# Sums of w1's column blocks made in DRAM by adding transfers, and a reordered opening and last output, in a two-layer attention and squared-ReLU kernel

## The chip, the cores and the metric

The kernel runs on one core of a Trainium2 chip. The metric is the device time of one execution in microseconds. The matrix engine is called PE (its weight loads run on a track of their own, PEld), the vector engine DVE, the scalar engine ACT, GpSimd POOL, and SP is the engine whose queue issues nearly all transfers. The 16 DMA engines serve all queues.

## The reference

One block is applied twice to `x` (2048 tokens, 1024 features): local dilated attention and a squared-ReLU feed-forward, each on a layer-normalised input, with residuals and with the same weights in both layers.

```python
x = x + _A_ref(_layernorm(x), A_wqkv, A_wo)              # 32 heads of 32, window of 8, dilation 2
x = x + _B_ref(_layernorm(x), B_w1, B_b1, B_w2, B_b2)    # h = relu(x@w1+b1)**2 ; h@w2+b2, 3584 wide
# ... and both once more
```

Inside `_A_ref`, each token's query is multiplied with the keys of eight tokens (itself and every second one before it, where there is one), a softmax runs over the eight, and the values are summed with its weights; the result goes through `wo`.

## The kernel before

**Units.** The 2048 tokens are cut into four blocks of 512, and the two layers make eight units, `u` = 0 to 7 (unit 0 is the first block of layer 0). A unit goes through `SA` (layer norm and transposition), `SQ` or `SQ7` (q, k, v), `S2` (products of q and k on DVE, sums over a head on PE, exponentials on ACT, weights times v on DVE), `SW` or `SW7` (output projection, residual, second layer norm), `SF1` (first feed-forward matrix, ReLU, square) and `SF2` (second matrix, residual, output).

**Seven products.** Most matrix products are done in 2 by 2 blocks by Winograd's scheme, with seven block products where the plain form has eight. Three of the seven use blocks of the weight as they are (`RAW`: products 1, 2 and 4), and four use combinations of its blocks (`COMB`: products 5, 7, 6 and 3). The moving side has its combinations too (`rhs_combos`, made on DVE for each unit). `product` (L643 on) issues the eight matmuls of one block product; they have line 659. In it, product 1 goes into PSUM bank X; ACT copies X into Y (`seed_first`, L592), and both banks then take further products.

**Where the weight's combinations come from.** They are made once, when a weight is first used, and stored in DRAM scratch for the later units: `keep_wqkv` (DVE line 527) for q, k, v, `keep_w1` (line 676) for `w1`, `keep_w2` (line 453) for `w2`, `keep_wo` for `wo`. For `w1`, whose 3584 columns are seven column blocks `dp` = 0 to 6 (each holds 256 columns of either half), this happens in unit 0, in `SF1_plain`. There block 0 is multiplied in the plain form (lines 1225 and 1229), and blocks 1 to 6 in the seven-product form. For each block the raw weight (two transfers of 512 KB) is loaded, four DVE instructions make the four combinations `tv` in SBUF, SP stores each of them (256 KB) to the scratch tensor `sw`, and the products of unit 0 take the combinations from SBUF (`X<-T,tv` and `Z<-xnB,tv` in the rows). Units 1 to 7 load a block's four combinations from `sw` in one transfer of 1 MB. The order within a block is set by `AT`: product 1 first, then 5, 2, 6, 3, 7, 4, with the blocks staggered by seven places.

**Softmax of unit 0.** `prod` multiplies q and k for eight chunks of features (line 944, one tile `P` each), adds the tiles in a tree of a given depth (line 952), and PE sums the tree's roots over each head (line 959, 4 matmuls per root). The depth is `DEP0 = (2, 2)` for the two halves of unit 0 and 3 for all later units: depth 2 leaves two roots per half, depth 3 one. ACT takes the exponential into tile `e` (line 970). `av` multiplies the weights with v (line 1023) and adds the eight window positions in three steps (line 1030).

**Opening.** The four tiles of unit 0 are loaded in the order 0, 1, 3, 2, tiles 1 and 2 from ACT's queue (`XACT`) and the others from SP's. Tiles 0 and 1 get their statistics on DVE (`ln_first`, lines 787 and 789) and are normalised there (line 784); tiles 2 and 3 (`LNA`) get theirs on ACT (lines 742 and 746). PE transposes them (line 803), DVE copies the first two out of PSUM in two halves each (line 806), and then the first products for q and k start (line 882).

**Last output.** For the very last output tile (`out_tile` with `end`, line 1450) PE computes the two halves of the last bank one after the other, DVE adds the residual to each half, and SP stores each.

**Order of the work.** Every operation is given to a planner (`Plan`) with an engine, an assumed duration, its dependences and a priority. The planner simulates engines, buffers and DMA with assumed costs and issues everything in the order that comes out. `ORDER` is a list of seeds that shift priorities. On the chip, each engine and each queue then works strictly in that order, and an instruction that waits for a semaphore holds all behind it on its engine. Buffers are slots of fixed classes (`K8`, `K4`, `K2`, `K1`: the numbers of 8, 4, 2 and 1 KB slots).

Of the kernel before, what the change touches and what calls it, by code (L numbers as in the profile page):

```python
# [37 lines left out]
XACT = (1, 2)  # L38
# [10 lines left out]
DEP0 = (2, 2)  # L49
# [4 lines left out]
COMB = (5, 7, 6, 3)  # L54
RT = 4
LNA = (2, 3)
# [3 lines left out]
K8, K4, K2, K1 = 12, 5, 12, 8  # L60
# [65 lines left out]
class Plan:  # L126
# [45 lines left out]
    def schedule(self):  # L172
# [19 lines left out]
        def fits(o):  # L192
            if o.mb and len(landed) >= LANES and landed[-LANES] > t + 1e-9:
                return False
# [27 lines left out]
        landed = []  # L222
# [3 lines left out]
        while left:  # L226
            progress = False
            for e in engs:
# [13 lines left out]
                if o.mb:  # L242
                    dma_free = max(dma_free, end) + o.mb / DMA_MBS
                    end = dma_free
                    landed.append(end + o.lat)
# [84 lines left out]
class _Kernel:  # L330
# [20 lines left out]
    def setup(self):  # L351
# [24 lines left out]
        self.b2b = const.tile([128, D], BF, name="b2b")  # L376
        self.b2d = const.tile([128, BLK], F32, name="b2d")
# [10 lines left out]
        todo = {"k": [("k", 0), ("k", 1)], "qv": [("q", 0), ("q", 1), ("v", 0), ("v", 1)], "w1": list(range(self.NDP))}  # L388
        self.orders = {j: interleave(d) for j, d in todo.items()}
# [963 lines left out]
    def SF2(self, u):  # L1353
# [73 lines left out]
        for q in range(2):  # L1427
            add(X[q], q, 1)
# [168 lines left out]
```

## Time and profile before

| what | value |
|---|---|
| median of three runs | 1133.62 us (1131.38 to 1135.53) |
| the profiled execution: its time, and its span | 1133.11 us, 1131.4 us |
| PE busy | 1119.1 us, 99% |
| DVE busy | 991.6 us, 88% |
| ACT busy | 814.4 us, 72% |
| POOL busy | 1.8 us |
| moved by DMA | 362.35 MB, mean 320 GB/s |
| granted PE clock | 1.00 |

The span is the time from the first to the last instruction or transfer of the profiled execution; its time is 1.7 us longer. "Busy" is the union of an engine's instructions. Matmuls are pipelined, so one row's mean duration (273 ns for 256 columns) is longer than the distance from one to the next (0.87 us for eight of them). The profile is of one execution; the table's median is of three others.

### The profile page before, as it was taken

To read this page: it belongs to the slowest core of one execution; us is meant where nothing else is said; L and a number is where in the kernel's file an instruction comes from. 1 tells how busy PE (TensorE), PEld (TensorE's weight loads), DVE (VectorE), ACT (ScalarE), POOL (GpSimd) and SP (SyncE) were. 2 spreads that over 40 slices of the span, in tenths; PEclk is the share of its full clock that TensorE was granted. 3 is DMA by queue.
4 is the path that set the end of the run, shared out by engine and by line. 5 is a ranking of instruction groups with operands and counts; after the bars stand their busy time and mean duration, and the time that the engine had idled before them with its cause. 6 is when DMAs were issued, how large, how long until landed. Compare 5 with 4: busy or idle time off the path is not lost.

```text
span 1131.4 us, 20642 instructions
## 1 busy us (share of the span) xinstructions
PE 1119.1 (99%) x7856; PEld 770.6 (68%) x7903; DVE 991.6 (88%) x1527; ACT 814.4 (72%) x1631; POOL 1.8 (0%) x8
## 2 busy tenths in 40 slices
PE   9999999999999999999999999999999999999998
PEld 6645764678746887468864788557884678845864
DVE  6999999999996999969999699997999799996341
ACT  7747996568975799556994669937798378933961
POOL 0000000000000000000000000000000000000000
PEclk9999999999999999999999999999999999999999
DMA  9956899999899988999879997899969999589881
GB/s 369 288 190 204 269 326 327 337 356 375 345 362 361 330 358 310 297 392 330 355 288 346 399 365 271 296 381 364 395 212 351 374 363 388 197 297 341 340 302 62
DMA packets 137022, 362.35 MB, mean 320 GB/s; under 512 B 67418, under 2 KB 68570, under 8 KB 116570
## 3 DMA queue, kind: packets, MB, share of 16 engines
q1 hardware_dynamic: 136634, 360.50, 90.9%
q8 instruction: 62, 1.02, 0.4%
q10 hardware_dynamic: 288, 0.52, 0.1%
q14 instruction: 38, 0.31, 0.1%
HBM read 314.84 MB, written 31.46 MB: 306 GB/s over the span
## 4 chain that ended last, share of the span: by engine, by line
PE 92%; ACT 5%; DMA 2%; issue 1%; DVE 0%; ACTq 0%; DVEq 0%; SPq 0%
PE X L659 26%; PE X L1382 15%; PE Z L659 13%; PE Z L1382 7%; PE Y L659 7%; PE pq L882 6%; PE py L481 4%; PE Y L1382 4%; PE py L1078 4%; PE X L1149 3%; PE Z L1149 2%; PE lg L959 1%; DMA w<-in_B_w_dram 1%; PE Y L1149 1%; DMA xt<-xs 1%; ACT r L1317 1%
## 5 line engine op out<-in xcount | busy, mean ns | idle before, releaser
L659 PEld LDWEIGHTS <-w 128*128 128x128 bf16 (+1 forms) x4904 | 479.6, 98 | 71.3 <-DMA w<-sw 1.2
L1382 PEld LDWEIGHTS <-r 128*128 128x128 f16 x1183 | 115.7, 98 | 136.5 <-issue 1.7
L1382 PE MATMUL X<-w,r 128*128 128x512 f16 (+2 forms) x784 | 176.1, 377 | 1.6 <-ACT yxa L1051 1.3
L944 DVE TENSOR_TENSOR P<-q,k 128x2048 f16<-128x2048 f16 x128 | 154.3, 1221 | 2.4 <-ACT q L622 0.9
L659 PE MATMUL X<-T,w 128*128 128x256 f16 x1224 | 154.2, 273 | 0.3 <-ACT u L1286 0.3
L1023 DVE TENSOR_TENSOR pr<-pb,v 128x4096 f16<-128x4096 f16 x64 | 146.2, 2293 | 0.5
L952 DVE TENSOR_TENSOR P<-P,P 128x2048 f16<-128x2048 f16 x110 | 133.3, 1215 | 0.1
L1317 ACT ACTIVATE r<-rr 128x1024 f16<-128x1024 f16 x110 | 124.2, 1147 | 0.2
L1030 DVE TENSOR_TENSOR pr<-pr 128x2048 f16<-128x2048 f16 (+1 forms) x128 | 117.7, 947 | 0.0
L659 PE MATMUL X<-TA,w 128*128 128x256 f16 x864 | 107.2, 273 | 0.1
L882 PE MATMUL pq<-xnA,w 128*128 128x256 f16 (+1 forms) x512 | 86.1, 326 | 0.2 <-ACT k L887 0.2
L592 ACT COPY Y<-X 128x512 f32<-128x512 f32 x115 | 70.3, 611 | 19.8 <-PE X L659 15.3
L1296 ACT CAST y<-Z 128x512 f16<-128x512 f32 x110 | 70.3, 655 | 7.3 <-PE Z L659 7.1
L882 PEld LDWEIGHTS <-w 128*128 128x128 bf16 x512 | 49.9, 98 | 32.6 <-issue 0.7
L1300 DVE TENSOR_TENSOR rr<-u,y 128x512 f16<-128x512 f16 x110 | 45.5, 419 | 25.2 <-ACT y L1296 16.6
L1323 ACT ACTIVATE rr<-Y,b1T 128x256 f16<-128x256 f32 x110 | 54.6, 536 | 4.9 <-PE Y L659 4.3
L659 PE MATMUL X<-xnB,w 128*128 128x256 f16 x440 | 56.1, 273 | 0.1
L659 PE MATMUL Y<-xnB,w 128*128 128x256 f16 x440 | 56.0, 273 | 0.0
L614 ACT CAST yq<-Z 128x512 f16<-128x512 f32 x72 | 41.5, 586 | 19.7 <-PE Z L659 19.7
L1323 ACT ACTIVATE rr<-X,b1T 128x256 f16<-128x256 f32 x110 | 55.6, 570 | 0.0
L1051 ACT CAST yxo<-X 128x512 f16<-128x512 f32 x27 | 15.4, 586 | 55.5 <-PE X L1382 55.5
L610 ACT CAST u<-X 128x512 f16<-128x512 f32 x72 | 41.5, 586 | 18.6 <-PE X L659 18.1
(166 smaller groups left out, 1684.6 us busy)
## 6 DMA issues: line engine op xcount, KB each, us to landing
w<-sw SPq DMA_DIRECT2D x49, 1024.0 KB, 9.1
w<-tw SPq DMA_DIRECT2D x56, 896.0 KB, 6.7
w<-in_B_w_dram SPq DMA_DIRECT2D x42, 896.0 KB, 5.3
w<-in_B_w_dram SPq DMA_DIRECT2D x35, 1024.0 KB, 9.8
w<-in_A_wqkv_dram SPq DMA_DIRECT2D x32, 1024.0 KB, 10.1
w<-sqv SPq DMA_DIRECT2D x24, 1024.0 KB, 10.5
w<-in_B_w_dram SPq DMA_DIRECT2D x28, 512.0 KB, 6.3
w<-sk SPq DMA_DIRECT2D x12, 1024.0 KB, 8.2
```

What stands on the lines that cost most here:

```text
L592: self.p.add("ACT", act(512), lambda: self.nc.scalar.copy(Y[:], X[:]), [(X, 0)], [(Y, 0)], UP, name="u")
L659: nc.tensor.matmul(bank[:, a, :], lw[:, k, a * 128:(a + 1) * 128], rhs(k), start=(start and k == 0 and a == 0), stop=(k == 3), skip_group_ ...
L882: nc.tensor.matmul(pq[:, t0 * HB:t1 * HB], w[:, c0 // 2 % 2, kd // 4, kd % 4, c0 % 2 * 128:c0 % 2 * 128 + 128], xnT[:, 2 * t0:2 * t1, kd, ...
L944: nc.vector.tensor_tensor(cur[:], q[:, c, None, hb * HB:(hb + 1) * HB].to_broadcast([128, W, HB]), _win_ap(k[:, c, :], HALO + hb * HB, HB) ...
L952: nc.vector.tensor_tensor(other[:], other[:], cur[:], ALU.add)
L1023: p.add("DVE", dve(4096), lambda pr=pr, ch=ch: nc.vector.tensor_tensor(pr[:], pb[:].unsqueeze(1).to_broadcast([128, 2, W, HB]), _win_ap2(v ...
L1030: nc.vector.tensor_tensor(dst, pr[:, :, 0:n, :], pr[:, :, n:2 * n, :], ALU.add)
L1149: nc.tensor.matmul(bank[q][:], left(j, q), right(j), start=start and j == 0, stop=j == h - 1, skip_group_check=True)
L1296: p.add("ACT", act(512), lambda: nc.scalar.copy(y[:], bank[:]), [(bank, 0)], [(y, 0)], 1.5, name="y")
L1317: p.add("ACT", 0.955, lambda: nc.scalar.activation(out=r2[:, f:f + 2, :].rearrange("p a t -> p (a t)"), in_=r[:].rearrange("p a m t -> p ( ...
L1323: p.add("ACT", 0.36, lambda a=a: nc.scalar.activation(out=r[:, a, 0, :], in_=bank[:, a, :], func=ACTF.Relu, bias=self.b1T[:, f + a:f + a + ...
L1382: nc.tensor.matmul(banks[q][:, lo:hi], left(jj, q), w[:, j, lo:hi], start=(start and jj == 0), stop=(jj == h - 1), skip_group_check=True)
```

## The change

It has these parts.

1. **Signs.** The seven-product scheme is rewritten so that all combinations of weights are sums. Product 1 goes into bank Y, and ACT writes its negative into X (`seed_minus`); some copies on ACT get a scale of -1, and some additions on DVE become subtractions.
2. **Adding transfers.** The host appends to `w1` (and to `wqkv`) six raw blocks per column block, in the order of `SUM`. For the blocks 3, 4, 5 and 6 of `w1` (`DM`), `make` issues four transfers each from POOL's queue: a copy of four raw blocks (1 MB) into the block's scratch, an adding transfer of two blocks (512 KB) onto the first two, one of 256 KB that adds the second to the third, and one of 256 KB that adds the third to the fourth. Each waits for the one before it. The blocks are staggered: step t - i of block i is issued at place t, and a place's transfers also wait for the first transfer of the block two places earlier. All wait for `go`, a small copy on POOL that reads the exponentials of unit 0's first half.
3. **Unit 0's feed-forward.** For blocks 3 to 6 `keep_w1` makes nothing; the products of unit 0 take the combinations from a 1 MB load of the scratch (`combos`). For blocks 0 to 2, and in `keep_w2`, two of the four sums are made by one DVE instruction into a pair tile, which is stored as one (`w1`) or two transfers (`w2`).
4. **DVE additions in `av`.** Six instructions for a pair of tiles become four over the same elements.
5. **Depth.** `DEP0` becomes (3, 3).
6. **Opening.** All four tiles are loaded from SP's queue; tile 2 gets its statistics and its normalisation on DVE, so only tile 3 stays on ACT; the second halves of the transposed tiles 0 and 1 are copied out of PSUM by ACT; the ordering constraints between the first DVE instructions change.
7. **Last output.** The residual is added by PE (a matmul with the identity); the two last halves are then copied out, one by DVE and stored from SP's queue, the other by ACT and stored from ACT's queue.
8. **Slots and order.** `K4` 5 to 6, `K2` 12 to 11, `K1` 8 to 7, and a new `ORDER`.

The core of the diff:

```diff
-XACT = (1, 2)
+XACT = ()
-DEP0 = (2, 2)
+DEP0 = (3, 3)
-COMB = (5, 7, 6, 3)
+COMB = (7, 5, 6, 3)
+SUM = ((0, 0), (1, 0), (0, 0), (0, 1), (1, 0), (1, 1))
+DM = (('w1', 3), ('w1', 4), ('w1', 5), ('w1', 6))
+AHEAD = 2
+POOL_ISSUE, POOL_LAT, MK_COPY, MK_ADD = 0.8, 3.0, 1.15, 1.9
-LNA = (2, 3)
+LNA = (3,)
+CPA = (1,)
+TAIL = True
-K8, K4, K2, K1 = 12, 5, 12, 8
+K8, K4, K2, K1 = 12, 6, 11, 7
...
+    def make(self, blocks, after=()):
...
+            def fn():
+                self.nc.gpsimd.dma_start(dst(), src(), **({} if op is None else {"accum_op": op, "max_dma_last_dim": 4096}))
+            return lambda after: p.add("POOL", POOL_ISSUE, fn, r, w, self.nxt(), after, mb=mb * (MK_COPY if op is None else MK_ADD), name="mk", lat=POOL_LAT)
...
+            return [step(0, 4, lambda: src[:, 0:4096], ()), step(0, 2, lambda: src[:, 4096:6144], (), ALU.add),
+                    step(2, 3, lambda: self.scr[job][d][:, 1].rearrange("p k n -> p (k n)"), [(key, 1)], ALU.add),
+                    step(3, 4, lambda: self.scr[job][d][:, 2].rearrange("p k n -> p (k n)"), [(key, 2)], ALU.add)]
...
+        chains = [rows(d) if job == "w2" else columns(job, d) for job, d in blocks]
+        heads = [after] * AHEAD
+        for t in range(len(chains) + max(map(len, chains)) - 1):
+            for i in range(len(chains)):
+                if 0 <= t - i < len(chains[i]):
+                    op = chains[i][t - i](heads[-AHEAD])
+                    if t == i:
+                        head = op
+            heads.append([head])
...
     def keep_w1(self, dp, w):
...
+        if ("w1", dp) in DM:
+            return self.combos("w1", dp) if dp >= PLAIN1 else None
...
+    def combos(self, job, d):
+        w = Buf("8K", "w", [128, 4, 4, 256], F16)
+        key = (job,) + (d if isinstance(d, tuple) else (d,))
+        self.dma(lambda: w[:], lambda: self.scr[job][d][:], [(key, i) for i in range(4)], [(w, 0)], 4 * 0.256, name="w")
+        return w
...
+    def seed_minus(self, X, Y):
+        self.p.add("ACT", act(512), lambda: self.nc.scalar.activation(out=X[:], in_=Y[:], func=ACTF.Identity, scale=-1.0), [(Y, 0)], [(X, 0)], UP, name="u")
...
+            if DM and u == 0 and hb == GO and EARLYGO:
+                st["go"] = p.add("POOL", 0.2, lambda: nc.gpsimd.tensor_copy(self.go[:], e[:, W - 1, 0:1]), [(e, W // 2 - 1)], [("go", 0)], 0.0, name="go")
...
-                for n in (4, 2, 1):
-                    for pr, ch in prs:
-                        def half(pr=pr, ch=ch, n=n):
...
+                big = prs[0][0]
+                for i, (pr, ch) in enumerate(prs):
+                    op = p.add("DVE", dve(2048), lambda pr=pr, big=big, i=i: nc.vector.tensor_tensor(
+                        big[:, :, 4 * i:4 * i + 4, :], pr[:, :, 0:4, :], pr[:, :, 4:8, :], ALU.add), [(pr, 0)], [(big, 0)], self.nxt(), name="avt")
...
+                half = lambda big, lo, n: big[:].rearrange("p c (g w) t -> p c g (w t)", g=2)[:, :, :, lo * HB:(lo + n) * HB]
+                p.add("DVE", dve(2048), lambda big=big: nc.vector.tensor_tensor(half(big, 0, 2), half(big, 0, 2), half(big, 2, 2), ALU.add),
+                      [(big, 0)], [(big, 0)], self.nxt(), name="avt")
...
+                    if split and half and q and TAIL:
+                        xr = xm[3]
+                        self.pe(1, lambda: nc.tensor.matmul(banks[1][:], self.ident[:], xr[:, 0:BLK], start=False, stop=False, skip_group_check=True),
+                                [(xr, 0)], [(banks[1], 0)], name="pp")
...
+        if end and TAIL:
+            for i in range(2):
...
+                p.add("ACT" if i else "DVE", act(HB) if i else dve(HB, False), lambda a=a, c=c, i=i: (nc.scalar.copy if i else nc.vector.tensor_copy)(o()[:, c], py[:, a]),
+                      [(py, i)], [(xm, (db, i))], -100.0, name="xo")
+                self.dma(lambda c=c: dst[:, c], lambda c=c: o()[:, c], [(xm, (db, i))], [(cell, (db, i))], 0.07, prio=-10.0, eng="ACT" if i else "SP")
+            return
...
         self.S2(0, DEP0)
+        if DM:
+            self.make(DM, [self.state[0]["go"]])
```

More of the change, by code (lines that the diff above doesn't have):

```diff
@@ L192, in fits @@
         def fits(o):
-            if o.mb and len(landed) >= LANES and landed[-LANES] > t + 1e-9:
+            mine = landed[o.eng == "POOL"]
+            n = 4 if o.eng == "POOL" else LANES
+            if o.mb and len(mine) >= n and mine[-n] > t + 1e-9:
                 return False
@@ L244, in schedule @@
                     end = dma_free
-                    landed.append(end + o.lat)
+                    landed[o.eng == "POOL"].append(end + o.lat)
                 out.append((t, len(out), o))
@@ L505, in w2_rhs @@
             lo, hi = half * h, (half + 1) * h
-            r = [(("tw", i), j0) for j0 in range(0, 2 * h, 2) if j0 < hi and j0 + 2 > lo]
+            r = [(("tw", i), half)] if "w2" in DM else [(("tw", i), j0) for j0 in range(0, 2 * h, 2) if j0 < hi and j0 + 2 > lo]
             self.dma(lambda: b[:, :h, :], lambda: self.tw[i][:, lo:hi, :], r, [(b, 0)], h * 0.13, name="w")
@@ L981, in norm, with go @@
                       ec, ec, self.nxt(), name="mask")
+            def go():
+                if DM and u == 0 and hb == GO and not EARLYGO:
+                    st["go"] = p.add("POOL", 0.2, lambda: nc.gpsimd.tensor_copy(self.go[:], ri[:, 0:1]), [(ri, 0)], [("go", 0)], 0.0, name="go")
             if u in DEN:
```

222 lines of the change are left out of this document (135 added, 87 removed), and 16 rows, old and new, of the table ORDER.

## The prediction

> **What bounds the kernel now.** I read the page's busy shares and its chain first, then PE's waits, then a division of the span at PE's first and last useful matmul (columns: stretch, length, then busy time of PE, PEld, DVE, ACT and POOL, granted clock, DMA share, GB/s).
>
> ```profile
> span 1131.4 us, 20642 instructions
> PE 1119.1 (99%) x7856; PEld 770.6 (68%) x7903; DVE 991.6 (88%) x1527; ACT 814.4 (72%) x1631; POOL 1.8 (0%) x8
> PE 92%; ACT 5%; DMA 2%; issue 1%; DVE 0%; ACTq 0%; DVEq 0%; SPq 0%
> ```
>
> ```profile
> 0.00:10.07 10.07, 7.27 (x36) 3.16 (x37) 5.85 (x19) 4.21 (x9) 1.76 (x8) 1.00 0.83 306
> 10.07:1127.20 1117.13, 1111.85 (x7822) 767.41 (x7867) 984.62 (x1506) 810.20 (x1623) 0.00 (x0) 1.00 0.92 321
> 1127.20:1131.40 4.20, 0.00 (x0) 0.00 (x0) 1.09 (x3) 0.00 (x0) 0.00 (x0) 1.00 0.20 62
> ```
>
> ```profile
> PE X L1382 <- ACT yxa L1051: 1.3, 1, 1.3
> PE Z L659 <- ACT rr L1323: 0.9, 1, 0.9
> PE X L659 <- ACT u L1286: 0.3, 1, 0.3
> PE pq L882 <- ACT k L887: 0.2, 1, 0.2
> ```
>
> The chain is PE. Between 10.07 and 1127.20 PE is idle for 1117.13 - 1111.85 = 5.3 us, of which named waits are 1.3 + 0.9 + 0.3 + 0.2 = 2.7; the rest are gaps too short to be listed. DVE, at 88%, ends almost no wait. So a DVE instruction saved is worth nothing by itself. What can be won is PE work, the 10.07 us before the first product, the 4.20 after the last, and part of the 5.3; what can be lost is PE's supply. The profiled execution took 1133.11 us, 1.7 more than its span; the sum starts from it. The median of the runs shown, 1133.62, is 0.5 longer. About 0.3% (3.4 us: 1130.2 to 1137.0 around the median) is what a measurement of this kernel can tell from no change.
>
> **The change part by part.**
>
> ```profile
> 38.55 0.43 PE lg L959 x2
> 50.66 0.86 PE lg L959 x4
> ```
>
> Depth: unit 0 has two halves with two roots of 4 matmuls each, afterwards one root, so 8 of these matmuls go. By the chain's rows one is 0.86 / 4 = 0.215 us: -1.7. PE is never late for work there, so it comes off the end. The price is one more tree addition per half on DVE. The last output adds one matmul with the identity: +0.2.
>
> ```profile
> 5.94 0.69 DVE L787 BATCH_NORM_STATS2 st<-x 128x6 f32<-128x512 bf16 x1 [0.37 <-DMA x<-in_A_x_dram]
> 8.67 1.49 DVE L806 COPY xnA<-pt 128x512 f16<-128x512 f16 x4
> 10.07 5.40 PE L882 MATMUL pq<-xnA,w 128*128 128x256 f16 x48
> 13.37 0.55 DVE L755 TENSOR_SCALAR xn<-x,sm 128x1024 f16<-128x1024 bf16 x1 [3.21 <-ACT sm L750]
> ```
>
> Opening: tile 1's statistics wait 0.37 us for a load that shares the DMA engines with three others; issued second on one queue it should come before the last two, against one more issue ahead of the weights on SP's queue. Four copies at a pitch of 1.49 / 4 = 0.37 us then stand between the transposes and the first product; two go to ACT, beside DVE's, which takes one pitch or a little less off. Together 0 to -1.0, if ACT were slow +0.3; I take -0.6. Tile 2's statistics and norm (about 2.5 us by rows L787 and L755, with its copy) go to DVE, into its idle 3.21 us before 13.37; without that cover, the first P would start later and DVE's work, not PE's.
>
> ```profile
> 1121.13 6.07 PE X L1382 x35
> 1127.23 0.42 DVE xm L1450
> 1127.65 0.33 DVEq L1592
> 1127.98 0.34 DVE xm L1450
> out_dram<-xm SPq DMA_DIRECT2D x2, 64.0 KB, 1.6
> ```
>
> Last output: two DVE instructions stand one behind the other from 1127.23 to 1128.32. On two engines with two queues the second starts with the first and is stored at once: -0.67 by rows 0.33 and 0.34 if ACT's copy is no longer than DVE's 0.42; bounds 0 and -0.8; I take -0.6. The store's 1.6 us stays.
>
> ```profile
> L676 DVE TENSOR_TENSOR tv<-w x14: 679/688/695, 100.7 to 151.8; 128x1024 f16<-128x1024 bf16 x14
> L1030 DVE TENSOR_TENSOR pr<-pr 128x2048 f16<-128x2048 f16 x64 | 77.1, 1214 | 0.0
> L1030 DVE TENSOR_TENSOR pr<-pr 128x1024 f16<-128x1024 f16 x64 | 42.4, 681 | 0.0
> L1030 DVE TENSOR_TENSOR o<-pr 128x512 f16<-128x512 f16 x64 | 25.3, 417 | 0.3 <-PE Z L659 0.3
> ```
>
> DVE: 16 combinations of 0.688 are no longer made, -11.0 in unit 0. In `av` two instructions of 0.681 become one of 1.214, and two of 0.417 one of 0.681: 0.30 saved for each of 32 groups, -9.6 over the kernel. The pairs and the deeper tree (+2.4) cancel roughly. Some 18 us less in all, where PE waits for nothing: 0 directly. It lets tiles reach ACT and PE earlier, and DVE is the engine that the planner must fit PE's work around. With that and a new order I take 1.0 of the 5.3 us of gaps: bounds -2.7 (all named waits gone) and +3 (twice as many; a new order meets the chip's durations as any other does, the named waits here being what the old order missed).
>
> Signs: scale -1 is in the same ACT instruction, and the moved seed has the same place; at worst an instruction of 0.5 us becomes 0.6. ACT is 72% busy and waits for PE oftener than PE for it: 0. SP no longer issues 16 stores, and issues 4 loads: 0.
>
> **The adding transfers.** POOL issues no transfer before, so their cost is bounded by rows of others (issues with size and time to landing; then PE's demand).
>
> ```profile
> w<-in_A_wqkv_dram SPq DMA_DIRECT2D x32, 1024.0 KB, 10.1
> sw<-tv SPq DMA_DIRECT2D x28, 256.0 KB, 3.9
> 39.56 2.05 ACT L970 ACTIVATE e<-lg 128x512 bf16<-128x512 f32 x4
> 129.56 1.04 PE L659 MATMUL Z<-T,tv 128*128 128x256 f16 x8
> 153.07 1.04 PE L659 MATMUL Z<-T,tv 128*128 128x256 f16 x8
> ```
>
> ```profile
> 43.00:57.00 14.00, 14.00 (x71) 6.63 (x70) 14.00 (x17) 8.24 (x19) 0.00 (x0) 1.00 1.14 307
> 57.00:70.00 13.00, 13.00 (x66) 6.31 (x65) 13.00 (x13) 7.20 (x14) 0.00 (x0) 1.00 0.54 198
> 70.00:85.00 15.00, 15.00 (x71) 6.77 (x70) 15.00 (x17) 5.74 (x11) 0.00 (x0) 1.00 0.49 175
> 85.00:100.00 15.00, 14.89 (x70) 6.82 (x70) 15.00 (x21) 11.33 (x25) 0.00 (x0) 1.00 0.26 79
> 100.00:113.00 13.00, 13.00 (x109) 9.17 (x108) 13.00 (x23) 9.52 (x22) 0.00 (x0) 1.00 1.00 348
> ```
>
> The start is the end of unit 0's first exponentials, 41.6, and one tree addition later with depth 3: about 43. Four blocks staggered by one place need seven places. The deadlines: the two rows of PE are the first product with a combination of block 3 (129.56) and of block 6 (153.07). The load before them lands in some 10 us, so block 3 must be done by 119, four places after 43 (19 us each), and block 6 by 143, seven places (14.3 us each). A place lasts at least what a store of 256 KB takes, 3.9, and, if a 1 MB transfer is always in it, 10.1; an addition that reads its target back could double that to 20. I take 8, nearer to the 1 MB row, because a 1 MB copy is in four of the seven places and the engines are half free: the last sum is there at 43 + 56 = 99. In volume, four blocks are 8.4 MB, or 12.6 with the additions' targets read back; at the 400 GB/s that loads reach, the five stretches leave 1.3 + 2.6 + 3.4 + 4.8 + 0.7 = 12.8 MB. So it fits before 113, hidden under PE's work on unit 1's q and k, without much room if the readback counts in full. Cost 0; ends 0 and +10.
>
> On DMA: Bandwidth & Descriptors, section "Issuing engines are not separate DMA queues", the Trainium skill says that transfers from SP, ACT and GpSimd end up on the same 16 DMA engines and interleave. By that rule, loads under way between 43 and 57, where the share is 1.14, would be slowed by the copies, and those between 57 and 100 hardly; by the rows, the sum stays as it is unless the copies also hold back the block loads of 100 to 113, which is the late chain below.
>
> **Sum:** -1.7 + 0.2 - 0.6 - 0.6 - 1.0 + 0 = -3.7; 1133.1 - 3.7 = 1129.4.
>
> **The rivals.**
>
> *The gaps stay or grow.* The certain part is -1.7 + 0.2 - 0.6 - 0.6 = -2.7, and a new order with gaps as long as before or up to 3 us longer gives 1130.4 to 1133.4: no change that can be told. For it: four waits in the old order came although PE is dense everywhere. Against it: DVE is lighter by 18 us.
>
> *The chain of adding transfers is late (slower).* Place: SP's queue at the first or last of the four combination loads. SP holds behind that load every later load of unit 0's feed-forward and unit 1's x tiles, until POOL's transfer has landed; PE starves once its loaded buffers are used. It decides from 14.3 us a place, and each us above costs up to 7 at block 6: 15.4 us a place bring 1129.4 + 7.7 = 1137.1, the edge of slower; 20 us would bring some 40. For it: the share of 1.14 at the start, 1.00 after 100, and places with up to 2 MB in four transfers at once. Against it: 57 to 100 is half empty, and 8 us is little more than half of 14.3.
>
> *The additions in `av` lose their rate.* The new views have four dimensions and could run at double the time, 2.4 instead of 1.214 for three of a group's four: about +3.4 us in each of 32 groups. In units 0 and 1, where DVE is at 100% (stretches above), 8 groups make +27 against 14 saved, and PE would wait for about 13: 1142. Against it: the innermost runs are 256 to 512 elements, no shorter than in the rows quoted, which are strided in tile and window too.
>
> **How the numbers follow.** The forecast, faster by more than 0.3%: 0.52. Gaps: 0.20, no change. A late chain: 0.20, of which 0.05 stays below 1137. Lost rate: 0.03, slower. Others (ACT's scaled copies late, slots short): 0.05, slower. So faster 0.52, same 0.25, slower 0.23. Low end: all bounds at their best, -1.7 + 0.2 - 1.0 - 0.8 - 2.7 = -6.0, 1127.1. High end: a late chain just past its point of decision, 1138. The forecast's own range is 1127.1 to 1130.2.
>
> **What would show it.** Right: 64 matmuls on line 959 instead of 72; first product before 10.07, near 9.5; the two last copies starting together and the span's tail under 4.20; POOL's last addition landing near 99 and in any case before 119 for block 3 and 143 for block 6; no PE wait on a scratch load between 120 and 160; the merged additions at 1.2 and 0.7 us; PE's idle time between first and last product near 4.3. Wrong: an SP queue that waits tens of us for POOL's transfer, loads of 43 to 57 landing far above 10 us with PE waiting, or new waits for ACT across the later units, where no part of the change but signs, slots and order is at work.

## The result and the profile after

The changed kernel is slower. Its median is 1148.08 us (1142.30 to 1150.19, six executions), the kernel before, measured beside it, took 1134.39 us (six executions). The ratio is 1.0117 with a 95% interval of 1.0102 to 1.0132, so about 13.3 us on 1134. The forecast was 1129.4 us, in a range of 1127.1 to 1138.0. The profiled execution took 1148.25 us.

From the page of the kernel after, its span, the busy shares, the chain that ended last, and the row of POOL's queue `q0` (packets, MB, time as a share of 16 DMA engines' span):

```profile
span 1146.5 us, 20510 instructions
PE 1121.5 (98%) x7850; PEld 770.1 (67%) x7896; DVE 982.8 (86%) x1441; ACT 815.4 (71%) x1626; POOL 14.6 (1%) x25
q0 software_dynamic: 2304, 8.39, 3.2%
PE 78%; DMA 10%; DVE 6%; ACT 3%; issue 1%; SPq 0%; DVEq 0%; ACTq 0%
```

DVE's work fell from 991.6 to 982.8 us, about half of what was forecast, and ACT's stayed. The chain is no longer PE nearly alone: 10% of it is DMA, where it was 2%. The span divided at PE's first and last product (columns as in the prediction):

```profile
0.00:9.51 9.51, 7.17 (x35) 3.08 (x36) 6.44 (x20) 4.80 (x10) 1.76 (x8) 1.00 0.76 261
9.51:1142.84 1133.33, 1114.30 (x7815) 767.00 (x7860) 975.95 (x1421) 810.19 (x1616) 12.88 (x17) 1.00 0.95 325
1142.84:1146.45 3.61, 0.00 (x0) 0.00 (x0) 0.42 (x1) 0.37 (x1) 0.00 (x0) 1.00 0.23 73
```

Both ends got shorter, 9.51 instead of 10.07 and 3.61 instead of 4.20. Between them PE is idle for 1133.33 - 1114.30 = 19.0 us, where it was 5.3. Its waits name most of that; these are the ones used below (in all, times, longest):

```profile
PE pq L965 <- DMA xnA<-xn: 8.0, 1, 8.0
PE Y L740 <- DMA w<-in_B_w_dram: 2.5, 2, 1.9
PE Y L740 <- ACT X L672: 2.1, 2, 1.1
PE pq L965 <- DMA w<-in_A_wqkv_dram: 1.2, 1, 1.2
PE Z L740 <- DMA w<-sw: 0.2, 1, 0.2
```

The last row is the sums that the adding transfers make: PE hardly waits for them. It waits once, for 8.0 us, for a transposing transfer that the prediction didn't speak of: the fourth and last tile of unit 1's normalised tokens (`xnA<-xn`, from SP's queue), and then for the raw blocks of `w1`. Three views around the first of these: stretches of 5 us, two of the kernel before and then three of the kernel after; SP's, POOL's and PE's instructions of the kernel after in order of time; and the time from issue to landing of this transposing transfer, in the kernel before (9.6) and after (18.8).

```profile
45.00:50.00 5.00, 5.00 (x27) 2.39 (x25) 5.00 (x6) 3.85 (x10) 0.00 (x0) 1.00 1.28 140
55.00:60.00 5.00, 5.00 (x24) 2.25 (x23) 5.00 (x5) 3.58 (x7) 0.00 (x0) 1.00 1.08 387
```

```profile
50.00:55.00 5.00, 5.00 (x29) 2.65 (x27) 5.00 (x9) 2.41 (x5) 1.45 (x3) 1.00 1.38 296
55.00:60.00 5.00, 1.01 (x6) 0.29 (x3) 5.00 (x8) 0.62 (x2) 0.00 (x0) 0.91 1.10 35
60.00:65.00 5.00, 0.97 (x3) 0.43 (x4) 5.00 (x4) 0.00 (x0) 0.72 (x2) 0.50 1.08 402
```

```profile
45.14 6.29 SPq L849 DMA_TRANSPOSE xnA<-xn  x1
50.19 1.26 POOL L447 DMA_DIRECT2D sw<-in_B_w_dram  x2
64.03 6.23 PE L965 MATMUL pq<-xnA,w 128*128 128x512 f16 x16 [8.02 <-DMA xnA<-xn]
64.28 1.40 POOL L447 DMA_DIRECT2D sw<-in_B_w_dram  x2 [12.83 <-DMA sw<-in_B_w_dram]
```

```profile
xnA<-xn SPq DMA_TRANSPOSE x1, 9.6
```

```profile
xnA<-xn SPq DMA_TRANSPOSE x1, 18.8
```

SP issues the transposing transfer at 45.14, POOL its first two copies of 1 MB at 50.19. Both are done together at about 64. From 55 to 60 the DMA engines are recorded as busy all the time (1.10) and move 35 GB/s. That isn't a bandwidth that is shared; it is a stretch in which almost nothing moves. A transposing transfer moves little by itself too, but not for as long: in the run without transfers below, the stretch of this transfer is 54 to 56, with 141 and 97 GB/s, and in the kernel before 45 to 50 has 140 GB/s. When PE has waited, its clock is granted at 0.50 (60 to 65), so that the first 16 matmuls take 6.23 us; a run below shows sixteen of them in 3.62.

### The profile page after: what moved, and what is told of

Read it like the earlier page. It is cut to its first block, busy times and chain, and to the rows that moved or that the text cites. A ratio compares the mean times of both kernels' runs of the same rounds, so it can differ in the third digit from the quotient of the medians.

```text
span 1146.5 us, 20510 instructions
## 1 busy us (share of the span) xinstructions
PE 1121.5 (98%) x7850; PEld 770.1 (67%) x7896; DVE 982.8 (86%) x1441; ACT 815.4 (71%) x1626; POOL 14.6 (1%) x25
## 3 DMA queue, kind: packets, MB, share of 16 engines
q0 software_dynamic: 2304, 8.39, 3.2%
## 4 chain that ended last, share of the span: by engine, by line
PE 78%; DMA 10%; DVE 6%; ACT 3%; issue 1%; SPq 0%; DVEq 0%; ACTq 0%
PE X L740 17%; PE X L1481 13%; PE Z L740 12%; PE Y L740 12%; PE Z L1481 6%; PE py L552 4%; DMA w<-in_B_w_dram 4%; PE pq L965 4%; PE Y L1481 3%; PE X L1243 3%; PE py L1172 2%; DMA xnA<-xn 2%; DVE P L1035 1%; PE Z L1243 1%; DVE P L1027 1%
## 5 line engine op out<-in xcount | busy, mean ns | idle before, releaser
L740 PEld LDWEIGHTS <-w 128*128 128x128 f16 (+1 forms) x5032 | 491.8, 98 | 79.0 <-DMA w<-in_B_w_dram 3.7
L740 PE MATMUL X<-T,w 128*128 128x256 f16 x1288 | 162.5, 273 | 0.1
L740 PE MATMUL Y<-xnB,w 128*128 128x256 f16 x880 | 110.2, 273 | 4.6 <-DMA w<-in_B_w_dram 2.5
L1119 DVE TENSOR_TENSOR pr<-pr 128x2048 f16<-128x2048 f16 x64 | 78.1, 1220 | 0.1
L1395 ACT ACTIVATE y<-Z 128x512 f16<-128x512 f32 x110 | 70.3, 657 | 5.4 <-PE Z L740 5.2
L740 PE MATMUL Y<-xnA,w 128*128 128x256 f16 x576 | 73.8, 273 | 0.0
L672 ACT ACTIVATE X<-Y 128x512 f32<-128x512 f32 x91 | 55.5, 610 | 19.4 <-PE Y L740 19.1
L690 ACT ACTIVATE u<-X 128x512 f16<-128x512 f32 x72 | 42.9, 597 | 19.9 <-PE X L740 18.7
L695 ACT ACTIVATE yq<-Z 128x512 f16<-128x512 f32 x72 | 42.6, 596 | 18.3 <-PE Z L740 18.0
L740 PE MATMUL Z<-T,w 128*128 128x256 f16 x424 | 54.8, 273 | 0.2 <-DMA w<-sw 0.2
## 6 DMA issues: line engine op xcount, KB each, us to landing
w<-sw SPq DMA_DIRECT2D x53, 1024.0 KB, 10.5
w<-in_A_wqkv_dram SPq DMA_DIRECT2D x32, 1024.0 KB, 10.5
```

Of the source, the lines that this page charges most:

```text
L672: self.p.add("ACT", act(512), lambda: self.nc.scalar.activation(out=X[:], in_=Y[:], func=ACTF.Identity, scale=-1.0), [(Y, 0)], [(X, 0)], U ...
L740: nc.tensor.matmul(bank[:, a, :], lw[:, k, a * 128:(a + 1) * 128], rhs(k), start=(start and k == 0 and a == 0), stop=(k == 3), skip_group_ ...
L1119: op = p.add("DVE", dve(2048), lambda pr=pr, big=big, i=i: nc.vector.tensor_tensor(big[:, :, 4 * i:4 * i + 4, :], pr[:, :, 0:4, :], pr[:, ...
L1395: p.add("ACT", act(512), lambda: nc.scalar.activation(out=y[:], in_=bank[:], func=ACTF.Identity, scale=by), [(bank, 0)], [(y, 0)], 1.5, na ...
```

## The experiments

Two theories stood at the start. **A:** the loss is the collision, packets of a second queue between those of a transposing transfer. **B:** the loss is volume: the adding transfers, with their targets read back, take more of the DMA engines than is free before unit 0's feed-forward needs its loads. Others came up on the way: the half clock, and the reordered opening. In all edits but the last two the order of the work, and so the seeds' plan, stays that of the kernel after, apart from the operations that the text says are moved. Differences in us below are ratios against the kernel before, measured beside each run, times 1134.

**No transfers at all.** This kernel leaves out the sums of blocks 3 to 6: unit 0 and all later units load block 0's sums in their place, so sizes and counts stay. The work of every engine but POOL stays as well.

```diff
-                self.nc.gpsimd.dma_start(dst(), src(), **({} if op is None else {"accum_op": op, "max_dma_last_dim": 4096}))
+                pass
...
+        e = 0 if (job, d) in DM else d
```

> The changed kernel in the same order, but POOL issues none of the 16 copies and adding transfers; the loads of the sums of blocks 3 to 6 take block 0's sums instead, which DVE makes in unit 0, so the products of those blocks are with the wrong weights while sizes and counts stay. Theory A (the transfers are the cause): no wait above 1 us near 56, full clock throughout, and the 4.1 us idle at 121 to 136 go too: 1148.2 - 8.0 - 2.8 - 4.1 = 1133. Theory B (the new order is the cause): 1145 or more, with the wait near 56 still there.

Measured: 1134.91 us, ratio 1.0005 (0.9994 to 1.0017), +0.6 us. So the adding transfers cost 13.3 - 0.6 = 12.7 us, which is all of the loss, and the rest of the change gains nothing that can be told. So the forecast of a faster kernel would have failed without the transfers too; that is taken up below with the opening.

**The chain begun behind the transposing transfer.** POOL's small copy `go` reads the last transposed tile of unit 1 instead of the exponentials, and the transfers are issued after it.

```diff
+    held = [o for o in order[:at + 1] if o.name in ("go", "mk")]
+    keep = [o for o in order[:at + 1] if o.name not in ("go", "mk")]
...
+    return keep + held + order[at + 1:]
...
-                st["go"] = p.add("POOL", 0.2, lambda: nc.gpsimd.tensor_copy(self.go[:], e[:, W - 1, 0:1]), [(e, W // 2 - 1)], [("go", 0)], 0.0, name="go")
+                st["go"] = p.add("POOL", 0.2, lambda: nc.gpsimd.tensor_copy(self.go[:], self.state[1]["xnA"][:, 3, 0, 0:1].bitcast(BF)), [(e, W // 2 - 1)], [("go", 0)], 0.0, name="go")
```

> The changed kernel with its planned order kept, except that the small copy on POOL and the adding transfers behind it are issued behind the last transposing transfer of unit 1's input, and the small copy reads that transposed tile, so that the first block copy starts when it has landed. Theory A: the wait of 8.0 us and the half clock after it (2.8 us lost) come from the two block copies meeting that transposition; both vanish, the transposing transfer lands in about 10 us instead of 18.8, and what the adding transfers cost later (4.1 us idle at 121 to 136) stays or grows, since the sums end later: 1137 to 1143. Theory B: the new order itself runs out of work at 56, whatever the copies do: the wait stays within 2 us of 8.0 and the time at 1146 to 1150.

Measured: 1141.37 us, 1.0066 (1.0051 to 1.0081), +7.5 us. Of this kernel, the stretch of the former wait and the one of the block loads, its two largest waits, and the landing of its transposing transfers; then the stretch of the block loads in the run without transfers:

```profile
55.00:60.00 5.00, 5.00 (x29) 2.57 (x28) 4.63 (x8) 1.98 (x4) 1.80 (x3) 1.00 1.22 282
100.00:140.00 40.00, 34.77 (x245) 22.25 (x243) 34.70 (x48) 22.57 (x48) 4.06 (x5) 1.00 0.78 235
PE Y L750 <- DMA w<-in_B_w_dram: 3.8, 4, 1.5
PE Y L750 <- ACT X L682: 2.9, 2, 1.8
xnA<-xn SPq DMA_TRANSPOSE x2, 10.6
```

```profile
100.00:140.00 40.00, 39.88 (x307) 28.49 (x305) 40.00 (x55) 29.12 (x60) 0.00 (x0) 1.00 0.44 144
```

The wait at 56 is gone, with PE busy throughout and the clock at 1.00, and the last two transposing transfers land in 10.2 and 11.1 us (10.6 is their median). What stays is 5.2 us of idle PE between 100 and 140, for raw blocks of `w1` and for ACT's copies behind the products that they delay. The DMA engines are full where the blocks are loaded: their share is 1.04 to 1.07 in each of five stretches from 57 to 125, where it is 0.41 to 0.92 without transfers. Both theories hold a part.

**The same transfers without adding.** As above, but every transfer is a plain copy of the same size, so the kernel leaves out the sums (the scratch holds raw blocks).

```diff
-                self.nc.gpsimd.dma_start(dst(), src(), **({} if op is None else {"accum_op": op, "max_dma_last_dim": 4096}))
+                self.nc.gpsimd.dma_start(dst(), src(), **{})
```

> The run with the late start, with the 12 adding transfers replaced by plain copies of the same size, so blocks 3 to 6 are multiplied with raw column blocks instead of sums. Theory A (an addition costs the DMA engines about twice a copy's time, and this crowds the loads between 80 and 120): the software queue's share falls from 3.2% to about 1.9%, the chain's last landing moves from about 122 to 105, and PE's idle time at 100 to 140 falls from 5.2 us to below 2: 1137. Theory B (the copies alone crowd the loads, or waits in the chain do): at most 1 us less.

Measured: 1134.83 us, 1.0003 (0.9994 to 1.0013). The 7 us are gone with the adding, more than Theory A had forecast (1137). POOL's queue in the late kernel, then in this one, and this one's stretch from 100 to 140:

```profile
q0 software_dynamic: 2304, 8.39, 3.1%
```

```profile
q0 software_dynamic: 1792, 8.39, 2.1%
100.00:140.00 40.00, 39.88 (x305) 28.43 (x303) 40.00 (x55) 29.42 (x62) 1.05 (x2) 1.00 0.58 200
```

The bytes counted are the same. As a recorded time of all 16 engines, the plain copies take 2.1% of 1131.2 us = 23.8 us, 2.8 us per MB. With adding it is 3.1% of 1139.8 = 35.3 us. Half of the bytes (4.19 MB) are copies in both, 11.9 us, so the adding half takes 23.4 us, or 5.6 us per MB: twice a copy. In the section "Rules for kernel authors" of DMA: Bandwidth & Descriptors, the Trainium skill says that an accumulating transfer reads its destination and writes it later; the doubled time agrees with that. So B is shown, with its size: 6.9 us over the kernel without transfers, and the same bytes as copies cost nothing that can be told. One thing is not separated: `max_dma_last_dim` goes with the adding, so this run has fewer packets too (1792 instead of 2304), and how much of the doubled time is the adding and how much the larger number of packets stays open.

**Two plain copies alone**, in the place of the first two transfers and nothing after them, once from POOL's queue and once from ACT's (the four blocks use block 0's sums, as without transfers).

```diff
-                self.nc.gpsimd.dma_start(dst(), src(), **({} if op is None else {"accum_op": op, "max_dma_last_dim": 4096}))
+                if op is None and w[0][0] in (("w1", 3), ("w1", 4)):
+                    self.nc.gpsimd.dma_start(dst(), self.scr["k"]["k", 0][:].rearrange("p i k n -> p (i k n)"))
...
+        e = 0 if (job, d) in DM else d
```

> The run without transfers, plus two plain DRAM to DRAM copies of 1 MB (stored sums of k, no change of type, into scratch that nobody reads) issued by POOL where the changed kernel issues its first two block copies; the products of blocks 3 to 6 take block 0's sums. Theory A (copies from a second queue beside the transposing transfer): the last transposing transfer of unit 1's input lands in 15 us or more, DMA falls to some 40 GB/s for several us while its share stays at 1, and PE waits 5 to 9 us near 56: 1140 to 1147. Theory B (it takes the change of type or the adding transfers behind): landing near 10 us, no wait above 2 us, 1133 to 1136.

> As the run with two plain copies from POOL, but the two copies are issued from ACT's queue at the same place in the order. If any second queue beside the transposing transfer does it: the same slow stretch near 40 GB/s and a PE wait of 5 to 9 us, 1140 to 1147. If it takes POOL's software queue: landing near 10 us and 1133 to 1137.

Measured: POOL's queue 1145.89 us, 1.0096 (1.0066 to 1.0125); ACT's 1145.70, 1.0092 (1.0047 to 1.0137). So 2 MB of copies cost 10 us by themselves, and it isn't POOL's kind of queue that does it. The first ratio rests on two executions only, and the four of the second lie between 1140.8 and 1152.3. First the copies from POOL, PE's wait and a stretch, then those from ACT:

```profile
PE pq L967 <- DMA xnA<-xn: 8.4, 1, 8.4
55.00:60.00 5.00, 1.23 (x7) 0.39 (x4) 5.00 (x9) 0.85 (x2) 0.00 (x0) 0.87 0.03 14
```

```profile
PE pq L967 <- DMA xnA<-xn: 13.5, 1, 13.5
55.00:60.00 5.00, 1.31 (x7) 0.44 (x5) 5.00 (x8) 0.92 (x2) 0.00 (x0) 1.00 0.28 76
50.26 1.20 ACTq L448 DMA_DIRECT2D sw<-sk  x2
```

The signature is that of the kernel after: the same wait, the transposing transfer landing in 18.8 us (POOL) and 23.6 us (ACT) where it takes 10.9 without transfers, and a stretch of 5 us with 14 or 76 GB/s. How busy the engines count in it differs (0.03, 0.28, 1.10), so that column can't tell a stall from work here; the bytes moved can.

**The same two copies from SP's own queue**, behind the transposing transfer. `go` and the copies are moved behind it as in the late chain; against the run from POOL's queue, the copies' line is:

```diff
-                    self.nc.gpsimd.dma_start(dst(), self.scr["k"]["k", 0][:].rearrange("p i k n -> p (i k n)"))
+                    self.nc.sync.dma_start(dst(), self.scr["k"]["k", 0][:].rearrange("p i k n -> p (i k n)"))
```

> The run without transfers, plus the two plain 1 MB DRAM to DRAM copies of the runs two_pool and two_act, issued from SP's queue directly behind unit 1's last transposing transfer (blocks 3 to 6 take block 0's sums). Theory A (the transposing transfer is slowed by packets of another queue, between its own): on one queue the copies follow it, it lands in about 10.6 us and PE does not wait for it: 1134 to 1137. Theory B (two copies of 1 MB at this place cost by their volume): 1140 or more.

Measured: 1135.39 us, 1.0012 (0.9995 to 1.0028). Of this kernel, the transposing transfer, the copies' issue, the stretch behind it, and the median landing of the last two transposing transfers:

```profile
45.81 5.38 SPq L861 DMA_TRANSPOSE xnA<-xn  x1
54.10 1.20 SPq L458 DMA_DIRECT2D sw<-sk  x2
55.00:60.00 5.00, 5.00 (x29) 2.58 (x28) 4.65 (x7) 2.04 (x5) 1.06 (x1) 1.00 0.94 341
xnA<-xn SPq DMA_TRANSPOSE x2, 10.3
```

The copies are issued before the transposing transfer has landed (10.9 us after 45.81, at 56.7), yet they do no harm: same bytes, nearly the same place, another queue, 9 us less. It also excludes that the 2 MB would be too much there. So it is shown that copies on a second queue beside the transposing transfer cause the loss. That their packets go between its packets is the likely way, and no trace shows it. And one reservation stays: these copies come four microseconds later than those of POOL and ACT, behind four other transfers of SP's queue, so the run doesn't separate the queue from the time at which the copies move.

**Ordinary loads on a second queue.** No transfers, and the two loads of `wo` for unit 0, which SP issues between its transposing transfers, go out from ACT's queue.

```diff
+    held = [o for o in order[:at] if getattr(o.fn, "on_act", False)]
...
+    return order[:at] + held + order[at:]
```

> The run without transfers, with the two 1 MB loads of wo for unit 0 (HBM to SBUF) issued from ACT's queue beside unit 1's last transposing transfer, where SP issues them ahead of it in the other runs. If packets of any transfer on a second queue slow the transposition: landing at 14 us or more and a PE wait of 3 us or more, 1138 or more. If it takes copies from DRAM to DRAM: landing near 10 us or earlier, 1133 to 1136.

Measured: median 1143.74 us, 1.0079 (1.0054 to 1.0105), but in two lumps: two of eight executions took 1133.4 and 1135.9, six 1142.6 to 1146.1. The profiled one is the 1133.4, and shows no wait on `xnA`; its loads were issued at 45.08 and landed in 10.4 us. So moving two loads into SBUF to a second queue mostly costs the same 10 us, and sometimes nothing. No slow one was profiled, so that it was the same wait is likely and not shown, and what decides stays open. In the fast one the transposing transfer landed in 11.9 us with the loads beside it: a second queue alone doesn't do the harm each time.

**The half clock.** Forty matmuls on a tile of ones ahead of unit 1's first product keep PE busy over the wait.

```diff
+                    for _ in range(40):
+                        nc.tensor.matmul(pq[:], g, g[:, None, :].to_broadcast([128, 4, 128]), start=True, stop=True)
```

> The changed kernel with 40 matmuls of ones (512 columns, 8.6 us at full clock) ahead of unit 1's first product, in the bank that this product then overwrites. If the half clock of 10.24 us at 59.5 to 69.7 follows PE's idle time: the granted clock stays 1.00 and 16 matmuls of line 965 behind the wait take 3.5 us instead of 6.2: 1148.2 - 2.8 + 0.6 = 1146. If it has another cause (the DMA traffic, say): the clock still falls, 1148 to 1149.

Measured: 1149.91 us, 1.0145 (1.0128 to 1.0162). By the ratios that is 3 us more than the change, with intervals that just overlap, where 2 us less had been expected. The clock did stay at 1.00 there:

```profile
60.00:70.00 10.00, 10.00 (x48) 4.55 (x47) 6.92 (x5) 2.15 (x5) 2.76 (x4) 1.00 1.04 335
56.13 8.81 PE L969 MATMUL pq<-ones 128*128 128x512 f16 x40
64.78 3.62 PE L971 MATMUL pq<-xnA,w 128*128 128x512 f16 x16
100.00:140.00 40.00, 34.93 (x204) 19.39 (x203) 30.83 (x42) 21.12 (x48) 3.25 (x4) 0.91 1.00 288
```

The 16 matmuls take 3.62 us, not 6.23, so the half clock follows from the idle time before it. In "What's actually happening" of TensorE: Matmul & The Clock Gate, the Trainium skill says that an idle window of some 3.4 us halves the clock; the 8.0 us of idle and the 0.50 agree. But PE is idle for 5.1 us between 100 and 140 all the same. The same products begin 1.9 us earlier than in the kernel after at 101, and 2.35 us later at 144: between them PE waits 2.1 us for a normalised tile and 2.3 for raw blocks of `w1`, whose loads are issued 1.2 to 1.3 us later than in the kernel after, and the clock falls to 0.83 between 110 and 130.

**The opening.** Tiles 1 and 2 go back to ACT's queue, ahead of its table load, once in the kernel after and once in the one without transfers.

```diff
+        order.insert([i for i, o in enumerate(order) if o.name == "x"][3] + 1, tab)
...
-            (self.nc.sync if eng == "SP" else self.nc.scalar).dma_start(o if cast is None else o.bitcast(cast), src())
+            (self.nc.sync if eng == "SP" and not on_act else self.nc.scalar).dma_start(o if cast is None else o.bitcast(cast), src())
```

> The changed kernel with input tiles 1 and 2 issued from ACT's queue again, ahead of the table load, all else in the same order. Theory A: the weights leave SP's queue 0.9 us earlier and PE's wait of 1.24 us for them at 12.20 goes, less what tile 1 loses by sharing: 1147.2, with the first product between 9.5 and 10.1. Theory B: the weights' arrival is set by the volume ahead of them, not by the issue: 1148.2.

> The run without transfers (blocks 3 to 6 take block 0's sums), with input tiles 1 and 2 issued from ACT's queue ahead of the table load. In the run without transfers PE idles 2.24 us between 10 and 20, most of it for the weights. Theory A (one queue for all four tiles delays the weights): the idle time between 10 and 20 falls below 0.8, the first product moves from 9.5 to about 10, and the time falls by 1 to 1.5: 1133.6. Theory B (volume): no difference, 1134.9.

Measured: with the transfers 1150.70 us, 1.0144 (1.0120 to 1.0168), above what either theory gave; there the transposing transfer landed in 21.3 us and PE waited 10.9 us for it, so the run says nothing of the opening. Without them 1134.47, 1.0001 (0.9990 to 1.0012), to be set beside the kernel without transfers at 1.0005: the intervals overlap, no gain can be told. The stretch from 10 to 20 in the kernel before, in the one without transfers (with PE's wait), and in that one with ACT's queue:

```profile
10.00:20.00 10.00, 10.00 (x101) 9.00 (x99) 5.58 (x7) 9.84 (x26) 0.00 (x0) 1.00 1.02 399
```

```profile
10.00:20.00 10.00, 7.76 (x79) 6.66 (x77) 6.30 (x9) 5.60 (x16) 0.00 (x0) 1.00 1.03 411
PE pq L966 <- DMA w<-in_A_wqkv_dram: 1.8, 1, 1.8
```

```profile
10.00:20.00 10.00, 9.30 (x91) 8.04 (x90) 8.17 (x13) 7.57 (x20) 0.00 (x0) 1.00 1.03 408
```

By 20 us PE has begun 83 of the products for q, k and v (`pq`, 0.11 us each) before, 64 without transfers, 73 with ACT's queue, and 72 in the kernel after. (PE's busy time of the first 10 us is mostly products on a tile of ones, and says nothing.) The new opening begins sooner and then waits for weights; with the old queues back it waits less and begins later, at 10.76. As two executions with the same opening differ by 8 products (64 and 72), what the queues alone do isn't shown.

**Fewer blocks, and none, planned anew.** To see the parts without the transfers in a kernel that leaves nothing out, and half of the volume, two versions were planned again with the same seeds, both with the old opening: no blocks by adding transfers, and blocks 5 and 6 alone, begun late.

```diff
-XACT = ()
+XACT = (1, 2)
...
-DM = (('w1', 3), ('w1', 4), ('w1', 5), ('w1', 6))
+DM = ()
...
-LNA = (3,)
+LNA = (2, 3)
...
```

> The changed kernel without any adding transfer (DVE makes the sums of all six blocks, as before the change) and with the opening of before (tiles 1 and 2 from ACT's queue, tile 2 normalised on ACT, DVE's copies and constraints as before), planned anew with the same seeds. Theory A (transfers cost 13, the other parts are worth their matmuls and the shorter tail): 8 matmuls less, 1 more and 0.6 off the tail give -2.1 against before, 1131 to 1133, if the new plan's gaps are like before's. Theory B (what the other parts save is lost in gaps of any order not searched for): 1134 to 1138.

> The changed kernel with only blocks 5 and 6 made by adding transfers, begun behind unit 1's last transposing transfer, DVE making the other blocks' sums, with the opening of before, planned anew with the same seeds. Theory A (the late start costs by volume: 36 us of DMA time do not fit, 18 do): no PE wait on raw weights between 100 and 140 above 1 us, and the time within 2 of the run without transfers and the opening of before. Theory B (any adding transfer beside the loads delays them): half of the late run's 6.5 us remain, 1137.

Measured: 1175.42 and 1175.58 us, both 1.0359 (1.0335 to 1.0383). These runs failed as experiments, and they decide between the theories of neither. In the first, PE's largest waits are many short ones behind ACT (7.0 us in 5, 6.3 in 5), and the transposing transfer is issued at 52.97, so that PE waits for that too, with no second queue in play. That seeds found for one set of operations are an arbitrary order for another, and that this costs the 40 us, is the likely reason and not shown; no part of the change can be read from it.

No kernel beat the one before. The best one that still makes the sums in DRAM is the late chain, at 1.0066.

## Why the prediction was wrong

**The step that failed is "Cost 0; ends 0 and +10", the price of the adding transfers.** It took them to be hidden under PE's work. They cost 12.7 us, beyond its own upper end. Two mechanisms make it up, each seen by itself: the collision with the transposing transfer (10.3 us more with POOL's two copies than without), and the adding itself (6.9 us more with the late chain than without). As ratios they add up to 17.2, more than 12.7. The traces, where the order of PE's work is the same, show how the two follow each other. One group of 16 transpositions on PE (`pt`) stands between the first products of the feed-forward. Without transfers, in the late chain and in the kernel after it begins at (first number):

```profile
118.33 1.06 PE L885 MATMUL pt<-ident,xn 128*128 128x128 f16 x16
124.86 1.21 PE L894 MATMUL pt<-ident,xn 128*128 128x128 f16 x16
132.52 1.22 PE L884 MATMUL pt<-ident,xn 128*128 128x128 f16 x16
```

The last group of 8 transpositions before it, ahead of the first product that needs a block of `w1`, begins at 102.26, 103.96 and 111.99. So in the kernel after PE is 9.7 us behind at the group of 8, from the collision, and 14.2 at the group of 16: 4.5 come between, from the volume. In the late chain it is 1.7 and 6.5, and 4.8 come between. The volume thus costs nearly the same with and without the collision, and the 1.7 were lost before: that execution had a granted clock of 0.91 in its first 20 us and had begun 47 of the products `pq` where the one without transfers had 64. These are single executions (the spans differ by 15.1 us, 1146.5 and 1131.4); so the shares are about 10 and about 5 us, and no closer than that.

*The collision.* The prediction asked what the transfers would do to loads and to volume, and never which transfers in flight at 43 to 57 had PE's next products behind them. The trace of before held it: a transposing transfer is issued on SP's queue at 47.84 and lands in 9.6 us, at 57.4, and a group of products on `xnA` begins at 57.63, so there was hardly any slack. The Trainium skill's rule that it cited (DMA: Bandwidth & Descriptors, "Issuing engines are not separate DMA queues") says that the queues interleave on the same engines. It points the right way, and the prediction listed "loads of 43 to 57 landing far above 10 us with PE waiting" as a sign of being wrong; that is what came, on a transfer that was no load. But sharing doesn't give the size. Two copies need 5.9 us of all engines (2.1 MB at 2.8), and beside them the transposing transfer landed 7.9 (POOL) and 12.7 us (ACT) later than without; and from SP's queue the same copies cost nothing that can be told. In the section "Rules for kernel authors" of DMA: Bandwidth & Descriptors, the Trainium skill says that a transpose next to ordinary DMAs needs nothing. The row there is about what has to be serialized, and the runs here show a price in time.

*The volume.* The prediction found 12.6 MB to fit into 12.8 "without much room", and counted that as hidden. The doubt was the right one: the adding half takes twice the time of a copy, and all sixteen transfers together take 36.7 us of all engines in the kernel after (3.2% of 1146.5). In the prediction's own five rows, the share free from 57 to 113 is 13 x 0.46 + 15 x 0.51 + 15 x 0.74 + 0 = 24.7 us. So it overflows by 12 us, and plain copies (23.8) just fit, as the run without adding shows. In the changed order the share free from 57 to 125, by the run without transfers, comes to 26.2 us, and says the same. Free GB/s had counted 1.3 MB in the stretch at 1.14, where no engine was free.

**The late-chain rival** put the loss at the right object and the wrong place: SP held by sums that come late. A place took about 10.5 us, not 8 (seven from 50.19 to the last landing at 123.7, 8.8 us after the issue at 114.91), under the 14.3 from which it would decide. SP's queue waited for none of these transfers between 75 and 165, and PE waited 0.2 us on `w<-sw`. The deadlines held, and what was late was everything else that used the DMA engines. The start, forecast at 43, came at 50: the new order ends unit 0's first exponentials at 49.6, where they ended at 41.6 before, and the prediction took the old order's time for them, with one tree addition more.

**The sum's other terms.** The depth: 64 matmuls on `lg` as said. The rows are of the kernel after: that group, the additions in `av`, the two last copies, and the weights' first loads.

```profile
L1042 PE MATMUL lg<-P,grp 128*128 128x512 f16 x64 | 19.4, 379 | 0.0
L1119 DVE TENSOR_TENSOR pr<-pr 128x2048 f16<-128x2048 f16 x64 | 78.1, 1220 | 0.1
L1124 DVE TENSOR_TENSOR pr<-pr 128x2048 f16<-128x2048 f16 x32 | 39.1, 1222 | 0.2
L1126 DVE TENSOR_TENSOR o<-pr 128x1024 f16<-128x1024 f16 x32 | 22.0, 688 | 0.4 <-PE X L740 0.3
1142.86 0.42 DVE L1553 CAST xm<-X 128x256 bf16<-128x256 f32 x1 [0.70 <-PE X L1481]
1143.32 0.37 ACT L1553 CAST xm<-X 128x256 bf16<-128x256 f32 x1 [1.62 <-DVE xm L1553]
2.67 4.67 SPq L438 DMA_DIRECT2D w<-in_A_wqkv_dram  x8
```

The additions in `av` keep their rate (1.22 and 0.69), so that rival fell. The last output: 3.61 instead of 4.20, the -0.6 taken, but not by the way given, so the size is luck: ACT's copy still follows DVE's (1143.32, released by it) instead of starting beside it. The copies end 0.85 us after the last product where they ended 1.12 after it, and the other 0.3 is behind the copies.

The opening, taken at -0.6, is a term with the wrong sign in these traces. The first product did come 0.56 us sooner. But the prediction counted "one more issue ahead of the weights"; it is two tiles moved to SP's queue, and the weights start at 2.67 where they started at 1.72. PE then waits for them, 1.2 us here and 1.8 in the kernel without transfers, and by 20 us it is 11 and 19 products `pq` behind before, 1.2 and 2.1 us at 0.11 each. With the depth and the identity at -1.5, the tail at -0.6 and the opening at +1.2 to +2.1 the sum is -0.9 to 0.0, and the kernel without transfers measures +0.6 (-0.7 to +1.9). The gaps, taken at -1.0, gave nothing that shows in the time. In the kernel without transfers PE is idle for 4.5 us between its first and last useful product, 2.2 of them from 10 to 20; the 5.3 of before is from records that lack some 47 matmuls (7856 beside 7903 weight loads), so the two can't be set against each other closely. DVE became lighter by 8.8 us (991.6 to 982.8), not by some 18: the additions in `av` save 144.8 - 139.2 = 5.6 us by the groups' busy times, not 9.6, and tile 2's norm, which moved to DVE, had been left out of that sum. Nothing here contradicts that it is worth nothing directly: the kernel without transfers, with DVE as light, gained nothing that can be told.

## What to carry to other kernels

Before a transfer is moved to an idle engine's queue, look for a transposing transfer in flight at that time and for who waits at its end; here two copies behind it in the same queue, and copies begun after it had landed, cost nothing that can be told. Cost a transfer by the time it takes on the DMA engines (an adding one took twice a copy here) against the share that is free in the stretch where it must be done, and a rival found "without much room" isn't worth 0. Parts of a change whose order comes from a search can only be told apart with that order kept.

## What was not expected of the hardware

A transposing transfer with copies of a second queue beside it landed in 17.3 to 23.6 us in five kernels, and in 9.6 to 11.9 us in seven others; for 5 us the engines moved 14 to 76 GB/s, with a recorded share anywhere between 0.03 and 1.10. Copies from POOL's and from ACT's queue did it alike, copies from the transposing transfer's own queue didn't, and with two loads on ACT's queue six of eight executions lost as much. Adding transfers from DRAM to DRAM took 5.6 us of all 16 engines per MB, in more packets, plain copies 2.8, though both count the same bytes.
